# A spectral mixer and an ELU MLP on one core: unread matmuls in two start-up waits, batch 0 spread over more engines and queues, Bs reads put later in the order

## The chip, the core and the metric

The kernel runs on one core of a Trainium2 chip. The metric is the device time of one execution in microseconds, the median of several. A core has five engines with a queue each: TensorE (PE in the profile; PEld is its weight load), VectorE (DVE), ScalarE (ACT), GpSimd (POOL) and SyncE (SP). SP computes nothing here; it starts transfers. Each engine works through its instructions in the order in which the program gives them, and a wait at the head of a queue holds everything behind it. Transfers started by any engine are carried by the core's 16 DMA engines.

## The reference

```python
X = np.fft.rfft(x, axis=1)                  # x: 8 x 3008 x 256
Yr = Xr @ w_r - Xi @ w_i + b_r
Yi = Xr @ w_i + Xi @ w_r + b_i
Yr = np.sign(Yr) * np.maximum(np.abs(Yr) - 0.01, 0.0)     # softshrink, Yi alike
y = np.fft.irfft(Yr + 1j * Yi, n=3008, axis=1)
h = y.reshape(24064, 256) @ w_in            # w_in: 256 x 2048
g = np.where(h > 0.0, h, np.exp(np.minimum(h, 0.0)) - 1.0)
out = g @ w_out                             # w_out: 2048 x 256
```

## The kernel before

Two parts share the core. The first, the mixer, takes each of the 8 batches through a Fourier transform written as matmuls. Its pieces are called units. For one batch there are 8 A units (first transform stage, from a tile `xt` of the input into a bf16 tile `A`, two units to a tile), 6 X units (second stage, from `Z` to `XT`), 12 M units (the complex channel matmul, bias and softshrink, from `XT` to `Y`), 6 B units (`Y` to `Bz`) and 8 Y units (`Bs` to `yT`). A unit is a few matmuls into one PSUM tile and one evacuation of it; M has more behind it (`yb` on DVE, then `clip` and `Y`, on POOL or on ACT and DVE).

Between stages the data is transposed through DRAM: the tiles A are written to `DA` (four writes, one for every two A units) and read back as Z (12 reads), and the tiles Bz are written to `DB` (three writes) and read back as Bs (8 reads). Before the change all of these transfers are started by SP. Reads wait until the writes have landed. There are two buffers for A and two for Bz, three for Z, four for Bs, four for xt. So the evacuation of A unit 4 must wait until the write of A units 0 and 1 has landed, and that of A unit 6 for the write of units 2 and 3.

The second part is the MLP. It takes `yT` of a batch in 6 blocks of 512 columns (the last has 448), each in 8 steps, so a batch has 48 iterations (`PER`). Iteration i has `front(i)` (4 matmuls into `hps`, then an Exp on ACT), then whatever units the plan puts there, then `elu(i)` (two DVE instructions, to `gT`), then `back(i - 2)` (8 matmuls into `ps_o`; after a block's last step ACT copies the result and SP writes it out). All 8 Y units of a batch must be evacuated before the first iteration of that batch, since every Bs tile holds a part of every block.

The order is written out by hand. `plan(b)` fills the 48 iterations of batch b with X, M, B and Y units of batch b + 1 and A units of batch b + 2. Units in the loop share one PSUM tile (tag `fps`, one buffer), so a unit's matmuls wait until the unit before it has been evacuated. Batch 0 has no batch before it: its units run alone, ahead of the loop, as does the building of the transform tables `M1` to `M4` by iotas, DVE arithmetic and Sin on ACT. `plan(0)` also has to hold the A units of batch 1 (iterations 6 to 13), so it starts X of batch 1 late, at iteration 18, packs the rest, and puts all 8 Y units into iterations 45 to 47. For batches 1 to 6 (`mixed`) X starts at iteration 2, A0 stands at 24, B4 at 25, A1 and A2 at 26 and 27, B5 and all Bs reads at 28, A3 to A7 at 29 to 33 with the Z reads, and Y0 to Y7 at 38 to 45. Batch 6 has no A units, batch 7 no units at all.

Of the kernel before, what the change touches and what calls it, by code (L numbers as in the profile page):

```python
# [20 lines left out]
K1 = 24  # L21
# [4 lines left out]
def kernel(  # L26
# [88 lines left out]
    def unit_A(b, u, alone=False, on_dve=False):  # L115
# [15 lines left out]
        )  # L131
        if uu == 1:
# [3 lines left out]
            del A_of[b, ci], x_of[b, ci]  # L136

    def load_Z(b, g):
        Z = wk3.tile([P, 8, D], BF16, name="Z", tag="Z")
        for c in range(2):  # L140
            for h in range(2):
                r = h * 2 * K1 + c * K1 + 8 * g
                q = c * N2 + h * NH
                nc.sync.dma_start(Z[q : q + NH], DA_of[b][:, r : r + 8, :])
        Z_of[b, g] = Z
# [44 lines left out]
    def unit_B(b, v, alone=False, on_dve=False):  # L190
# [19 lines left out]
        )  # L210
        if v % 2:
            k0 = 8 * (v // 2)
            nc.sync.dma_start(DB_of[b][k0 : k0 + 8].rearrange("k p d -> p k d"), Bz[:])

    def load_Bs(b, w):
        Bs = wk4.tile([4 * K1, 8, D], BF16, name="Bs", tag="Bs")
        dv = DB_of[b].rearrange("k (c m) d -> (k c) m d", c=2)
        for h in range(2):
            n0 = h * NH + 8 * w
            nc.sync.dma_start(Bs[h * 2 * K1 : h * 2 * K1 + 2 * K1], dv[:, n0 : n0 + 8, :])  # L220
        Bs_of[b, w] = Bs

    def unit_Y(b, u, alone=False, on_dve=False):
# [6 lines left out]
        for j in range(8):  # L230
# [6 lines left out]
            psv[:, :, 0 : 2 * N1].rearrange("p n r -> p r n"), on_dve,  # L237
        )

    with tc.tile_pool(name="stagep", bufs=1) as stagep:  # L240
# [78 lines left out]
        r2 = stagep.tile([P, 2, 8, N2], F32, name="r2")  # L319
        for g in range(3):  # L320
            gs = slice(8 * g, 8 * g + 8)
# [9 lines left out]
            )  # L331
            for c in range(2):
                wrap(flat(v2[:, c, gs, :]), flat(r2[:, c]))
            for u in range(2 * g, 2 * g + 2):
                unit_A(0, u, alone=True)
            for c in range(2):
                nc.scalar.activation(
                    flat(M2[:, c, gs, :]), flat(v2[:, c, gs, :]), AF.Sin,
                    bias=0.0, scale=SIN_SCALE,
                )  # L340
        dume = stagep.tile([P, 1], F32, name="dume")
        nc.scalar.activation(dume[:], pcol[:], AF.Exp, scale=0.0)
        for u in range(6, 8):
            unit_A(0, u, alone=True, on_dve=(u == 7))
        for g in range(3):
            load_Z(0, g)

# [34 lines left out]
        nc.tensor.matmul(bb[:], lhsT=ones[:], rhs=brow[:], start=True, stop=True)  # L382
        nc.scalar.copy(bias_bc[:], bb[:])
        nc.gpsimd.tensor_copy(wcat_r[:, :, 0:D], w_r_f[:])
        nc.gpsimd.tensor_copy(wcat_r[:, :, D : 2 * D], w_i_f[:])
# [9 lines left out]
    def load_w(fp):  # L395
        f0 = fp * 2 * P
        wf = wk4.tile([P, 2, 2 * P], F32, name="w_in_f", tag="w_in_f")
        nc.sync.dma_start(wf[:], w_in_v[:, :, f0 : f0 + 2 * P])
        nc.gpsimd.tensor_scalar(
            w_in_s[:, :, f0 : f0 + 2 * P], wf[:], 2.0 / S, None, ALU.mult  # L400
        )
        nc.gpsimd.dma_start(w_out_r[:, 2 * fp : 2 * fp + 2, :], w_out_v[:, 2 * fp : 2 * fp + 2, :])


    unit_X(0, 0, alone=True)
    unit_X(0, 1, alone=True, on_dve=True)
    for i in range(2):
        unit_M(0, 0, i, alone=True)
    for i in range(2):
        unit_M(0, 1, i, alone=True, path="dve")  # L410
    unit_X(0, 2, alone=True)
    unit_X(0, 3, alone=True)
    for fp in range(4):
        load_w(fp)
    for i in range(2):
        unit_M(0, 2, i, alone=True, path="dve")
    unit_B(0, 0, alone=True)
    for i in range(2):
        unit_M(0, 3, i, alone=True)
    unit_B(0, 1, alone=True)  # L420
    unit_X(0, 4, alone=True)
    unit_X(0, 5, alone=True)
    for i in range(2):
        unit_M(0, 4, i, alone=True, path="dve")
    unit_B(0, 2, alone=True)
    for i in range(2):
        unit_M(0, 5, i, alone=True, path="dve")
    unit_B(0, 3, alone=True)
    unit_B(0, 4, alone=True)
    unit_B(0, 5, alone=True)  # L430
    for w in range(4):
        load_Bs(0, w)
    for fp in range(4, NPAIR):
        load_w(fp)
    for ci in range(4):
        load_x(1, ci)
    for u in range(8):
# [75 lines left out]

    def mixed(b, lead):

        r = [[] for _ in range(PER)]
        nxt = b + 1 < B
        seq = [
# [5 lines left out]
        ]  # L524
        t = lead
        for u in seq:
            if u[0] == "A":
                if not nxt:
                    t += 1
                    continue  # L530
                r[t].append(put("A", b + 1, *u[1:]))
            else:
                r[t].append(put(u[0], b, *u[1:]))
            if u == ("B", 5):
                for w in range(4):
                    r[t].append((load_Bs, (b, w)))
            if u == ("A", 7) and nxt:
                for g in range(3):
                    r[t].append((load_Z, (b + 1, g)))
            t += 1  # L540
        return r, t

    def plan(b):

        if b + 1 >= B:
            return [[] for _ in range(PER)]
        if b == 0:
            r = [[] for _ in range(PER)]
            for u in range(8):
                r[6 + u].append(put("A", 1, u))  # L550
            for g in range(3):
                r[13].append((load_Z, (1, g)))
            X = [put("X", 1, u) for u in range(6)]
            M = [[put("M", 1, q, i) for i in range(2)] for q in range(6)]
            Bu = [put("B", 1, v) for v in range(6)]
            seq = [
                [X[0]], [X[1]], [M[0][0]], [M[0][1]], [X[2]], [M[1][0]], [M[1][1]], [X[3]],
                [Bu[0]], [M[2][0]], [M[2][1], Bu[1]], [X[4]], [M[3][0]], [M[3][1], Bu[2]], [X[5]],
                [M[4][0]], [M[4][1], Bu[3]], [M[5][0]], [M[5][1], Bu[4]], [], [Bu[5]],
            ]  # L560
            t = 18
            for us in seq:
                r[t] += us
                t += 1
            for w in range(4):
                r[t - 1].append((load_Bs, (1, w)))
            for ci in range(4):
                r[15 + 4 * ci].append((load_x, (2, ci)))
            for u in range(8):
                r[t + u * 6 // 8].append(put("A", 2, u))  # L570
            for g in range(3):
                r[t + 5].append((load_Z, (2, g)))
            for u in range(8):
                r[PER - 3 + u * 3 // 8].append(put("Y", 1, u))
            return r
        r, t = mixed(b + 1, 2)
        for u in range(8):
            r[t + 4 + u].append(put("Y", b + 1, u))
        if b + 2 < B:
            for ci in range(4):  # L580
                r[3 + 4 * ci].append((load_x, (b + 2, ci)))
        return r

    n = B * PER
    todo = None
    for i in range(n + LAG):
        if i < n:
            if i % PER == 0:
                todo = plan(i // PER)
            h = front(i)  # L590
            for f, a in todo[i % PER]:
                f(*a)
            elu(i, *h)
        if i >= LAG:
            back(i - LAG)


# [28 lines left out]
```

## Time and profile before

| | us |
|---|---|
| median of 3 runs | 1074.23 (1072.34 to 1076.02) |
| the profiled execution, its own time | 1076.73 |
| span of its instructions | 1074.8 |
| PE busy | 956.4 (89%) |
| DVE busy | 829.5 (77%) |
| ACT busy | 630.7 (59%) |
| POOL busy | 259.4 (24%) |
| mean granted TensorE clock, share of 2.4 GHz | 0.95 |

The shares are means over the start-up, seven batches with units and one without, which have different limits. All rows are from that profiled execution; its times are counted from the span's start.

### The profile page before, as it was taken

The numbers are of one execution on the slowest core, as the hardware profiler recorded it, in microseconds if no ns is written. First come the engines' busy times: TensorE is split into PE (matmuls) and PEld (weight loads), VectorE is DVE, ScalarE is ACT, GpSimd is POOL, SyncE is SP. The second block draws the span as 40 slices with busy tenths as digits, with TensorE's granted clock in tenths as the row PEclk, the third lists the DMA queues.
The fourth block names the chain that finished last, engine by engine and source line by source line (L and its number), as shares of the span: only waits on it lengthen the run. The fifth ranks groups of instructions, "written<-read, shape, count | busy, mean of one in ns | idle before, by whom it ended". The sixth has DMA issues, their size and how long they took to land.

```text
span 1074.8 us, 16330 instructions
## 1 busy us (share of the span) xinstructions
PE 956.4 (89%) x6427; PEld 675.5 (63%) x6427; DVE 829.5 (77%) x932; ACT 630.7 (59%) x725; POOL 259.4 (24%) x270
## 2 busy tenths in 40 slices
PE   4648798679997999899997999899997999999997
PEld 2225575457665766577665766677665766676765
DVE  8326587528985899678985899768986888888887
ACT  4244565556675755666665756666565766565554
POOL 4415035203430055002530055101530034100000
PEclk9577899979998999999998999989999999999999
DMA  8538643641447133640536124640435211411011
GB/s 181 143 96 199 159 118 84 138 121 42 121 111 174 38 78 88 171 113 19 138 95 177 55 53 117 154 128 20 103 95 155 69 38 53 107 40 38 20 40 38
DMA packets 92784, 105.39 MB, mean 98 GB/s; under 512 B 5730, under 2 KB 83556, under 8 KB 89700
## 3 DMA queue, kind: packets, MB, share of 16 engines
q1 hardware_dynamic: 86436, 77.61, 26.4%
q0 software_dynamic: 6272, 26.74, 11.3%
q8 instruction: 50, 0.82, 0.3%
q14 instruction: 26, 0.21, 0.1%
HBM read 54.53 MB, written 49.81 MB: 97 GB/s over the span
## 4 chain that ended last, share of the span: by engine, by line
PE 69%; DVE 12%; ACT 8%; DMA 8%; issue 2%; SPq 1%; DVEq 0%; POOL 0%; ACTq 0%; POOLq 0%
PE hps L454 28%; PE ps_o L487 25%; PE mps L176 8%; DVE gT L465 8%; DMA DA<-A 6%; ACT Et L459 5%; DVE Et L463 3%; PE aps L124 3%; PE bps L200 2%; PE yps L231 2%; PE xps L155 2%; ACT A L113 1%; SPq L220 1%; DVE yb L181 1%; DMA xt<-in_x_dram 1%
## 5 line engine op out<-in xcount | busy, mean ns | idle before, releaser
L459 ACT ACTIVATE Et<-hps 128x1024 f32<-128x1024 f32 (+1 forms) x384 | 388.6, 1012 | 328.2 <-PE hps L454 325.6
L465 DVE SCALAR_TENSOR_TENSOR gT<-hps,Et 128x1024 fp32r<-128x1024 f32 (+1 forms) x384 | 461.8, 1203 | 34.9 <-DVE Et L463 0.5
L487 PE MATMUL ps_o<-w_out_r,gT 128*128 128x256 f32 (+1 forms) x3072 | 485.2, 301 | 0.7 <-DVE gT L465 0.7
L487 PEld LDWEIGHTS ps_o<-w_out_r,gT 128*128 128x128 f32 (+1 forms) x3072 | 416.2, 192 | 45.5 <-issue 10.2
L454 PE MATMUL hps<-yT,w_in_s 128*128 128x512 bf16 (+1 forms) x1536 | 399.4, 383 | 19.6 <-DVE gT L465 18.9
L463 DVE TENSOR_SCALAR Et<-Et 128x1024 f32<-128x1024 f32 (+1 forms) x384 | 280.7, 731 | 145.8 <-ACT Et L459 144.8
L184 POOL TENSOR_SCALAR clip<-yb 128x512 f32<-128x512 f32 x88 | 78.7, 894 | 590.9 <-DVE yb L181 590.5
L454 PEld LDWEIGHTS <-w_in_s 128*128 128x128 bf16 x1536 | 128.9, 99 | 138.5 <-issue 32.0
L185 POOL TENSOR_TENSOR Y<-yb,clip 128x512 bf16<-128x512 f32 x88 | 112.8, 1282 | 7.5
L124 PE MATMUL aps<-xt,M 94*96 94x512 f32 x128 | 55.0, 521 | 57.6 <-ACT A L113 44.1
L113 ACT CAST A<-aps 96x1024 bf16<-96x1024 f32 x63 | 62.9, 1003 | 55.1 <-DMA DA<-A 43.4
L181 DVE TENSOR_TENSOR yb<-mps,bias_bc 128x512 f32<-128x512 f32 x96 | 66.4, 691 | 26.6 <-PE mps L176 19.6
L176 PEld LDWEIGHTS <-XT 128*128 128x128 bf16 x384 | 38.3, 101 | 60.3 <-issue 14.6
L124 PEld LDWEIGHTS aps<-xt,M 94*96 94x96 f32 x128 | 21.4, 190 | 76.2 <-ACT A L113 57.9
L176 PE MATMUL mps<-wcat_r,XT 128*128 128x512 bf16 x192 | 61.2, 399 | 8.4 <-DVE yb L181 5.0
L176 PE MATMUL mps<-wcat_s,XT 128*128 128x512 bf16 x192 | 60.7, 399 | 0.0
L113 ACT CAST yT<-yps 128x752 bf16<-128x752 f32 x60 | 47.0, 784 | 14.5 <-PE yps L231 14.5
L113 ACT CAST Bz<-bps 128x1024 bf16<-128x1024 f32 x48 | 48.7, 1018 | 8.2 <-PE bps L200 8.2
L499 ACT COPY osb<-ps_o 128x512 f32<-128x512 f32 x96 | 50.8, 583 | 4.1 <-PE ps_o L487 4.1
L99 POOL DMA_DIRECT2D xt<-in_x_dram x64 | 44.0, 690 | 34.2 <-PE aps L124 34.0
L113 ACT CAST XT<-xps 128x1024 bf16<-128x1024 f32 x47 | 47.0, 1005 | 5.2 <-PE xps L155 5.2
L231 PE MATMUL yps<-M,Bs 96*128 96x94 bf16 x512 | 34.1, 217 | 15.7 <-DMA Bs<-DB 10.0
(69 smaller groups left out, 220.8 us busy)
## 6 DMA issues: line engine op xcount, KB each, us to landing
xt<-in_x_dram POOLq DMA_DIRECT2D x32, 640.0 KB, 6.1
out_dram<-osb SPq DMA_DIRECT2D x40, 512.0 KB, 3.1
DA<-A SPq DMA_DIRECT2D x32, 384.0 KB, 5.9
Z<-DA SPq DMA_DIRECT2D x96, 128.0 KB, 3.2
DB<-Bz SPq DMA_DIRECT2D x24, 512.0 KB, 3.2
Bs<-DB SPq DMA_DIRECT2D x64, 192.0 KB, 4.7
xt<-in_x_dram POOLq DMA_DIRECT2D x32, 112.0 KB, 5.7
out_dram<-osb SPq DMA_DIRECT2D x8, 384.0 KB, 2.6
```

What stands on the lines that cost most here:

```text
L113: nc.scalar.copy(dst, src)
L124: nc.tensor.matmul(ps[0 : 4 * K1, j, :], lhsT=M1[:], rhs=xt[:, 4 * uu + 2 * j : 4 * uu + 2 * j + 2, :], start=True, stop=True,)
L176: nc.tensor.matmul(ps[:, i, :], lhsT=XT[:, dt, c, o : o + P], rhs=wm[:, dt, :], start=(m == 0 and dt == 0), stop=(m == 1 and dt == 1),)
L181: nc.vector.tensor_tensor(yb[:], ps[:, i, :], bias_bc[:], ALU.add)
L184: nc.gpsimd.tensor_scalar(clip[:], yb[:], LAM, -LAM, ALU.min, ALU.max)
L185: nc.gpsimd.tensor_tensor(Y[:, i, :], yb[:], clip[:], ALU.subtract)
L231: nc.tensor.matmul(psv[:, j, 0 : 2 * N1], lhsT=Bs[:, j, dt * P : dt * P + P], rhs=M4[:], start=True, stop=True,)
L454: nc.tensor.matmul(hps[:, s, 0:nb], lhsT=w_in_s[:, dt, ft * P : ft * P + P], rhs=yT[:, dt, bs : bs + nb], start=(dt == 0), stop=(dt == 1),)
L459: nc.scalar.activation(Et[:, :, 0:nb], hps[:, :, 0:nb], AF.Exp)
L463: nc.vector.tensor_scalar(Et[:, :, 0:nb], Et[:, :, 0:nb], 1.0, -1.0, ALU.min, ALU.add)
L465: nc.vector.scalar_tensor_tensor(gT[:, :, 0:nb], hps[:, :, 0:nb], 0.0, Et[:, :, 0:nb], ALU.max, ALU.add)
L487: nc.tensor.matmul(po[q][0 : t1 - t0, i_ % 2, :], lhsT=gT[:, s, t0:t1], rhs=w_out_r[:, ft, :], start=(ft == 0 and i_ % 2 == 0), stop=(ft = ...
```

## The change

1. Start-up. In the table loop the A units of batch 0 alternate between ACT and DVE for their evacuation; units 6 and 7 are put ahead of the last Sins, and every unit writes its own half of the tile to DA. X units alternate likewise. The Z and Bs reads of batch 0 are started half by SP and half by ACT.
2. The M units of batch 0 alternate between the two softshrink paths. The MLP weights come in 4 large loads of `w_in`, into buffers of the loop's tiles, early, with the scaling done by DVE after unit B5, and 2 loads of `w_out`, started by POOL; `load_x` of batch 1 moves ahead of B3.
3. `idle_pe(n)` issues n matmuls whose result nobody reads: 20 ahead of X0, 22 ahead of Y0 of batch 0.
4. `plan` returns two lists. Units of `f1` stand where units stood; those of `f2` behind `back`. Bs reads stand in `f2` of the iteration of A4, Z reads in `f2` of the last A unit, and Y0 to Y7 at iterations 40 to 47 for all batches.
5. `plan(0)` gets a list of its own: X of batch 1 from iteration 17, some iterations with two units, A units of batch 2 spread over iterations 32 to 39.

```diff
+def load_Bs(b, w, engs=None):           # load_Z alike
+    engs = engs or (nc.sync, nc.sync)
...
+            engs[h].dma_start(Bs[h * 2 * K1 : h * 2 * K1 + 2 * K1], dv[:, n0 : n0 + 8, :])
...
+    def idle_pe(n):
+        ps = psO.tile([P, 512], F32, name="idle", tag="outp")
+        for _ in range(n):
+            nc.tensor.matmul(
+                ps[:], lhsT=M2[:, 0, 0:2, :].rearrange("p a b -> p (a b)"),
+                rhs=M2[:, 0, 0:8, :].rearrange("p a b -> p (a b)"), start=True, stop=True,
+            )
...
+            wrap(flat(v2[:, 0, gs, :]), flat(r2[:, 0]))
+            unit_A(0, 2 * g, alone=True)
+            unit_A(0, 2 * g + 1, alone=True, on_dve=True)
+            if g == 2:
+                unit_A(0, 6, alone=True)
+                unit_A(0, 7, alone=True, on_dve=True)
+            wrap(flat(v2[:, 1, gs, :]), flat(r2[:, 1]))
+            sines(g)
...
+    def both_M(q):
+        unit_M(0, q, 0, alone=True, path="pool")
+        unit_M(0, q, 1, alone=True, path="dve")
...
+    both_M(5)
+    load_w_out(1)
+    for ci in range(4):
+        load_x(1, ci)
     unit_B(0, 3, alone=True)
     unit_B(0, 4, alone=True)
-    unit_B(0, 5, alone=True)
+    unit_B(0, 5, alone=True, on_dve=True)
     for w in range(4):
-        load_Bs(0, w)
-    for fp in range(4, NPAIR):
-        load_w(fp)
-    for ci in range(4):
-        load_x(1, ci)
+        load_Bs(0, w, (nc.sync, nc.scalar))
+    for q in range(4):
+        nc.vector.tensor_scalar_mul(
+            w_in_s[:, :, q * FQ : q * FQ + FQ], w_in_f[q][:], 2.0 / S
+        )
+    idle_pe(22)
...
+            lead, pairs = 17, [
+                [("X", 0), ("X", 1)], [("M", 0, 0)], [("M", 0, 1)], [("X", 2), ("X", 3)],
+                [("M", 1, 0)], [("M", 1, 1)], [("M", 2, 0)], [("M", 2, 1), ("B", 0)],
+                [("X", 4), ("X", 5)], [("M", 3, 0)], [("M", 3, 1), ("B", 1)],
+                [("M", 4, 0)], [("M", 4, 1), ("B", 2)], [("M", 5, 0)], [("M", 5, 1), ("B", 3)],
+                [("A", 0)], [("A", 1), ("B", 4)], [("A", 2)], [("B", 5), ("A", 3)], [("A", 4)],
+                [("A", 5)], [("A", 6)], [("A", 7)],
+            ]
...
+        for t, us in enumerate(pairs, lead):
+            us = [u for u in us if n2 < B or u[0] != "A"]
+            at(t, *us[:1])
+            at(t, *us[1:], r=f2)
+            if ("A", 4) in pairs[t - lead]:
+                f2[t] += [(load_Bs, (n1, w)) for w in range(4)]
...
         for u in range(8):
-            r[t + 4 + u].append(put("Y", b + 1, u))
+            at(40 + u, ("Y", u))
```

In the order of SP's transfers, this is what stood around the Bs reads in the iterations of batch 1 before:

```order
L133 DMA DA<-A 96x8x256
L213 DMA DB<-Bz 128x8x256
L220 DMA Bs<-DB 48x2048 x8
L133 DMA DA<-A 96x8x256 x3
L144 DMA Z<-DA 32x2048 x12
```

And this is the same place after:

```order
L138 DMA DA<-A 96x8x256
L223 DMA DB<-Bz 128x8x256
L138 DMA DA<-A 96x8x256
L231 DMA Bs<-DB 48x2048 x8
L138 DMA DA<-A 96x8x256 x2
L534 DMA out_dram<-osb 128x4x256
L149 DMA Z<-DA 32x2048 x12
```

The second write of A (units 2 and 3) moved from behind the 8 Bs reads to ahead of them; the other two stay behind. On POOL's queue, start-up ends before with these rows, from the last two M units on its path to the loads of batch 1:

```order
L184 TENSOR_SCALAR clip<-yb 128x512
L185 TENSOR_TENSOR Y<-yb,clip 128x512
L399 TENSOR_SCALAR w_in_s<-w_in_f 128x2x256
L402 DMA w_out_r<-in_moe_w_out_dram 128x2x256
L399 TENSOR_SCALAR w_in_s<-w_in_f 128x2x256
L402 DMA w_out_r<-in_moe_w_out_dram 128x2x256
L399 TENSOR_SCALAR w_in_s<-w_in_f 128x2x256
L402 DMA w_out_r<-in_moe_w_out_dram 128x2x256
L399 TENSOR_SCALAR w_in_s<-w_in_f 128x2x256
L402 DMA w_out_r<-in_moe_w_out_dram 128x2x256
L99 DMA xt<-in_x_dram 80x2048
L99 DMA xt<-in_x_dram 14x2048
```

and after with these:

```order
L189 TENSOR_SCALAR clip<-yb 128x512
L190 TENSOR_TENSOR Y<-yb,clip 128x512
L434 DMA w_out_r<-in_moe_w_out_dram 128x8x256
L99 DMA xt<-in_x_dram 80x2048
L99 DMA xt<-in_x_dram 14x2048
```

The scalings of w_in, which waited for loads that SP starts behind the Bs reads, are gone from POOL, so nothing on its queue holds the loads of batch 1 back once the last clip is done.

## Rows read from the trace of the kernel before

**Rows 1.** Windows, one per batch, between first Exps; ACT instructions of L459 alone.
```profile
core 0: us, ACT busy (x), PEclk, DMA share, GB/s
89.33:243.91 154.58, 48.49 (x48) 0.90 0.53 130
243.91:367.06 123.15, 48.60 (x48) 0.97 0.40 102
...
735.23:856.76 121.53, 48.62 (x48) 0.99 0.37 97
856.76:968.88 112.12, 48.63 (x49) 1.00 0.20 57
968.88:1074.82 105.94, 48.48 (x48) 0.99 0.10 34
```

**Rows 2.** Windows of a few iterations each, cut at Exp starts; same columns.
```profile
89.33:103.20 13.87, 6.16 (x6) 0.76 0.77 177
968.88:981.46 12.58, 6.16 (x7) 1.00 0.12 38
973.07:1052.69 79.62, 39.05 (x38) 1.00 0.10 33
...
375.91:381.28 5.37, 2.06 (x3) 1.00 0.00 0
440.79:447.64 6.85, 3.08 (x4) 1.00 0.74 205
447.64:459.55 11.91, 2.05 (x3) 0.79 0.70 177
164.24:168.59 4.35, 1.02 (x1) 1.00 0.30 66
226.02:243.91 17.89, 2.75 (x3) 0.81 0.44 111
```

**Rows 3.** Waits: engine and line, what it waited for; us, times, longest.
```profile
ACT A L113 <- DMA DA<-A: 43.4, 8, 6.4
```

**Rows 4.** Timeline around one long wait, batch 2: start, us, instruction, idle before.
```profile
440.18 0.37 SPq L213 DMA_DIRECT2D DB<-Bz  x1
...
441.71 1.00 ACT L113 CAST A<-aps 96x1024 bf16<-96x1024 f32 x1
...
444.22 3.77 SPq L220 DMA_DIRECT2D Bs<-DB  x8
...
446.28 1.00 ACT L113 CAST A<-aps 96x1024 bf16<-96x1024 f32 x1
...
448.08 9.37 SPq L133 DMA_DIRECT2D DA<-A  x3
...
453.85 1.01 ACT L113 CAST A<-aps 96x1024 bf16<-96x1024 f32 x1 [5.18 <-DMA DA<-A]
```

**Rows 5.** DMA issues from 440 to 460 us: KB each, median us to landing.
```profile
Bs<-DB SPq DMA_DIRECT2D x8, 192.0 KB, 4.1
```

**Rows 6.** Windows of start-up, X0 to the last evacuation of B5, and its two parts.
```profile
core 0: us, PE busy (x) PEld busy (x) DVE busy (x) ACT busy (x) POOL busy (x), PEclk, DMA share, GB/s
33.32:72.78 39.46, 28.17 (x144) 12.00 (x144) 15.34 (x21) 15.97 (x19) 16.37 (x16) 0.67 0.35 93
33.32:55.08 21.76, 17.39 (x68) 7.45 (x69) 8.61 (x11) 6.55 (x8) 12.66 (x12) 0.50 0.51 132
55.08:72.78 17.70, 10.78 (x77) 4.55 (x75) 6.74 (x10) 9.42 (x12) 3.71 (x4) 0.89 0.16 44
```

**Rows 7.** Timeline of start-up: TensorE's last work ahead of X0, and X0 and X1.
```profile
27.16 1.41 PE L382 MATMUL bb<-brow,ones 1*128 1x512 f32 x2
...
33.32 1.87 PE L155 MATMUL xps<-M,Z 128*128 128x128 bf16 x16 [4.75 <-DMA Z<-DA]
```

**Rows 8.** The chain that ended last, 60 to 95 us: start, us, what.
```profile
62.24 1.88 PE mps L176 x4
...
72.78 3.22 DMA DB<-Bz
...
79.29 5.99 DMA Bs<-DB
```

**Rows 9.** The chain that ended last, 100 to 125 us.
```profile
107.43 11.81 DMA DA<-A
```

More of the change, by code (lines that the diff above doesn't have):

```diff
@@ L131, in unit_A @@
         )
-        if uu == 1:
+        if alone:
+            n0 = 4 * u
+            nc.sync.dma_start(
+                DA_of[b][n0 : n0 + 4].rearrange("n r d -> r n d"), A[:, 4 * uu : 4 * uu + 4, :]
+            )
+        elif uu == 1:
             nc.sync.dma_start(
@@ L319, with sines @@
         r2 = stagep.tile([P, 2, 8, N2], F32, name="r2")
+        def sines(g):
+            gs = slice(8 * g, 8 * g + 8)
+            for c in range(2):
+                nc.scalar.activation(
+                    flat(M2[:, c, gs, :]), flat(v2[:, c, gs, :]), AF.Sin,
+                    bias=0.0, scale=SIN_SCALE,
+                )
         for g in range(3):
@@ L331 @@
             )
[L332 to L340, printed above, removed]
+            wrap(flat(v2[:, 0, gs, :]), flat(r2[:, 0]))
[6 more added lines that the diff above has]
+            sines(g)
         dume = stagep.tile([P, 1], F32, name="dume")
         nc.scalar.activation(dume[:], pcol[:], AF.Exp, scale=0.0)
-        for u in range(6, 8):
-            unit_A(0, u, alone=True, on_dve=(u == 7))
         for g in range(3):
-            load_Z(0, g)
+            load_Z(0, g, (nc.sync, nc.scalar))
         ident_b = stagep.tile([P, P], BF16, name="ident_b")
@@ L393 @@
     w_out_v = moe_w_out.rearrange("(t p) e -> p t e", p=P).bitcast(F32R)
[L395 to L402, printed above, removed]
+    FQ = DFF // 4
+    w_in_f = []
@@ new lines, in load_w_in, with load_w_out @@
+    def load_w_in():
+        for q in range(4):
+            if q < 3:
+                wf = late3.tile([P, 2, FQ], F32, name="w_in_f", tag="Et")
+            else:
+                wf = late2.tile([P, 2, FQ], F32, name="w_in_f", tag="osb")
+            nc.sync.dma_start(wf[:], w_in_v[:, :, q * FQ : q * FQ + FQ])
+            w_in_f.append(wf)
+    def load_w_out(hh):
+        hf = slice(hh * NFT // 2, (hh + 1) * NFT // 2)
+        nc.gpsimd.dma_start(w_out_r[:, hf, :], w_out_v[:, hf, :])
+    def both_M(q):
+        unit_M(0, q, 0, alone=True, path="pool")
+        unit_M(0, q, 1, alone=True, path="dve")
@@ L405 @@
     unit_X(0, 0, alone=True)
     unit_X(0, 1, alone=True, on_dve=True)
[L407 to L410, printed above, removed]
+    load_w_in()
+    both_M(0)
+    load_w_out(0)
+    both_M(1)
     unit_X(0, 2, alone=True)
-    unit_X(0, 3, alone=True)
-    for fp in range(4):
-        load_w(fp)
-    for i in range(2):
-        unit_M(0, 2, i, alone=True, path="dve")
+    unit_X(0, 3, alone=True, on_dve=True)
+    both_M(2)
@@ L417 @@
     unit_B(0, 0, alone=True)
-    for i in range(2):
-        unit_M(0, 3, i, alone=True)
+    both_M(3)
     unit_B(0, 1, alone=True)
     unit_X(0, 4, alone=True)
-    unit_X(0, 5, alone=True)
-    for i in range(2):
-        unit_M(0, 4, i, alone=True, path="dve")
+    unit_X(0, 5, alone=True, on_dve=True)
+    both_M(4)
     unit_B(0, 2, alone=True)
-    for i in range(2):
-        unit_M(0, 5, i, alone=True, path="dve")
+    both_M(5)
+    load_w_out(1)
+    for ci in range(4):
+        load_x(1, ci)
@@ L428 @@
     unit_B(0, 3, alone=True)
     unit_B(0, 4, alone=True)
-    unit_B(0, 5, alone=True)
+    unit_B(0, 5, alone=True, on_dve=True)
     for w in range(4):
-        load_Bs(0, w)
-    for fp in range(4, NPAIR):
-        load_w(fp)
-    for ci in range(4):
-        load_x(1, ci)
+        load_Bs(0, w, (nc.sync, nc.scalar))
+    for q in range(4):
+        nc.vector.tensor_scalar_mul(
+            w_in_s[:, :, q * FQ : q * FQ + FQ], w_in_f[q][:], 2.0 / S
+        )
+    idle_pe(22)
     for u in range(8):
@@ L512, in put @@
         return ({"A": unit_A, "X": unit_X, "M": unit_M, "B": unit_B, "Y": unit_Y}[kind], (b, *a))
[L514 to L518, printed above, removed]
[5 rows of a table removed]
[L524 to L541, printed above, removed]
@@ L543, in plan, with at @@
     def plan(b):
+        f1 = [[] for _ in range(PER)]
+        f2 = [[] for _ in range(PER)]
         if b + 1 >= B:
-            return [[] for _ in range(PER)]
+            return f1, f2
+        n1, n2 = b + 1, b + 2
+        def at(t, *us, r=f1):
+            for u in us:
+                r[t].append(put(u[0], n2 if u[0] == "A" else n1, *u[1:]))
         if b == 0:
-            r = [[] for _ in range(PER)]
             for u in range(8):
-                r[6 + u].append(put("A", 1, u))
-            for g in range(3):
-                r[13].append((load_Z, (1, g)))
@@ L553, in plan @@
[L553 to L559, printed above, removed]
-            ]
-            t = 18
@@ L575, in plan @@
-            return r
-        r, t = mixed(b + 1, 2)
-        for u in range(8):
-            r[t + 4 + u].append(put("Y", b + 1, u))
[L579 to L582, printed above, removed]
+                f1[6 + u].append(put("A", 1, u))
+            f1[13] += [(load_Z, (1, g)) for g in range(3)]
+            lead, pairs = 17, [
[6 rows of a table added]
+            ]
+            xs = (15, 18, 21, 24)
+        else:
+            lead, pairs = 2, [[u] for u in (
[5 rows of a table added]
+            )]
+            xs = (3, 7, 11, 15)
@@ new lines, in plan @@
+        for t, us in enumerate(pairs, lead):
[4 more added lines that the diff above has]
+                f2[t] += [(load_Bs, (n1, w)) for w in range(4)]
+        if n2 < B:
+            f2[t] += [(load_Z, (n2, g)) for g in range(3)]
+            for ci in range(4):
+                f1[xs[ci]].append((load_x, (n2, ci)))
+        for u in range(8):
+            at(40 + u, ("Y", u))
@@ L588 @@
             if i % PER == 0:
-                todo = plan(i // PER)
+                f1, f2 = plan(i // PER)
             h = front(i)
-            for f, a in todo[i % PER]:
+            for f, a in f1[i % PER]:
                 f(*a)
@@ L595 @@
             back(i - LAG)
+        if i < n:
+            for f, a in f2[i % PER]:
+                f(*a)
 _INS = ['x', 'w_r', 'w_i', 'b_r', 'b_i', 'moe_w_in', 'moe_w_out']
```

31 lines of the change are left out of this document (12 added, 19 removed), and 10 rows, old and new, of tables (seq, xs).

## The prediction

> **What bounds the kernel now.** I began with the span cut into batches [rows 1]. Batch 7, which has no units, takes 105.94 us, and 38 of its iterations take 79.62 us, 2.095 each [rows 2]: that is the floor of the loop. A batch with units is not far above it where nothing goes wrong: batch 6, which lacks only the A units, takes 112.12. Batches 1 to 5 take 612.85 together (from 243.91 to 856.76, 122.57 each), batch 0 takes 154.58, and start-up 89.33. So three places hold what is left to get: start-up, batch 0, and about ten microseconds in each of five batches.
>
> The list of waits names the last: ACT, evacuating an A unit, waited 43.4 us in 8 waits for writes of A to DRAM [rows 3]. The timeline of one of them shows why [rows 4]. ACT has A unit 3 in its tile at 442.71 (start 441.71 and 1.00), and the write of that tile could start there. SP has the 8 Bs reads ahead of it, though, and these wait for the write of Bz that was started at 440.18; SP starts them from 444.22 to 447.99, and the write of A only at 448.08. It lands some 5.8 later, and unit 6, which needs that buffer, is evacuated at 453.85 after 5.18 idle. Two iterations take 11.91 in that stretch at a mean granted clock of 0.79, where undisturbed iterations with an A unit take 2.283 (6.85 for three) [rows 2]: the excess is 11.91 - 4.57 = 7.34. The clock loss of the restart is inside it.
>
> **The change, part by part.**
>
> *Batches 1 to 5.* The second write of A now stands ahead of the Bs reads, so it starts at about 442.7 on that timeline. Unit 6 can be evacuated one A iteration after unit 5, 446.28 + 2.28 = 448.56 [rows 2, 4]. That leaves 5.85 for a write that took 5.8 behind all eight reads; now it has only the tail of the Bz write ahead of it and the reads after it. I take the wait as gone. If nothing new appears, that is 5 x 7.34 = 36.7 off, 115.2 for a batch; batch 6 plus 8 A units at 2.283 - 2.095 each comes to 113.6, which agrees within 1.6. The upper bound of what is left: the write shares the engines with the Bs reads and lands with the last of them. These would start from 444.3 to 448.1 and land 4.1 later [rows 5], at 452.2; a wait of 3.6, and 3.6 x 7.34 / 5.18 = 5.1 with the clock loss, 25.5 over five. The writes of units 4 to 7 go behind the Bs reads, with nothing but the Z reads late by it, and X uses these from iteration 2 of the next batch, some 16 iterations on; the Bs reads themselves come one or two iterations later for a Y0 that moved two iterations later too.
>
> *The batch boundary.* Y7 now stands in iteration 47, and the next `front` needs its evacuation. No single Y there is shown. Nothing is the lower bound, as one unit beside `back` may be covered; the upper one is the end of batch 0, where 8 Y units in three iterations took 17.89 [rows 2], so 11.6 over 3 x 2.095, or 1.45 each. I take 0.3 at each of 6 boundaries, 1.8, near the low end because a single unit has no other unit to queue behind.
>
> *Batch 0.* With the same units and single Y units it should cost a clean batch, 115.2, with additions: the 8 A units of batch 1, 8 x 0.19 = 1.5; a start at a low clock, 13.87 for six iterations against 12.58 for the same six of batch 7 [rows 2], 1.3; and nine iterations with two units. A pair ahead of `back` (M and B) took 4.35 [rows 2]; M alone takes 2.685 (5.37 for two), and a light unit adds about 0.19, so 2.87 would be the price of no collision, and 1.48 is the excess. The second of a pair now stands behind `back`, whose matmuls cover part of the wait for the shared PSUM buffer, so I take 0.7, between the ends: 6.3. Sum: 124.3, 30.3 less than 154.58, with 118 and 131 as the ends. It assumes that the write of batch 1's first A tiles, 11.81 us at 107.43 [rows 9], gets short. It ran among the loads of x for batches 1 and 2, and the loads of batch 1 now start during start-up; with a landing of about 5.8, as above, three A iterations (6.85) cover it.
>
> *Start-up.* Three parts, the least certain ones. First, X0 begins at 33.32, behind TensorE's last matmul at 28.57 [rows 7]. Three more evacuations of about 1 us on DVE delay the last tables by about 3, to 31.6, and 20 unread matmuls come on top. A 512-column matmul took 0.47 at the half clock (1.88 for four) [rows 8], so 20 take 4.7 to 9.4, and the X units queue behind them on TensorE although Z has landed. I take 6: X0 at 37.6. The ends are 33.3 (the wait hides all) and 41.
>
> Second, from X0 to the last evacuation of B5, 39.46 [rows 6]. TensorE is busy for 17.39 at 0.50 and 10.78 at 0.89 of the clock, so 18.3 at full clock, and not busy for 11.3: M's second half waits for `yb`, the first M of a pair waits for XT. With X evacuated on two engines I take 10 of these, and a clock of 0.8, between the 0.67 of that stretch and full: 18.3 / 0.8 + 10 = 33. The ends are 28 (full) and 46 (half). So B5 is done at 70.6 instead of 72.78. Neither softshrink path nor the w_out load on POOL counts: POOL and ACT are busy for 16 of 39 us. The rule in the Trainium skill (TensorE: Matmul & The Clock Gate, Part 1) is that the throttled clock is the default and activity releases it. The half clock ahead of 55.08, with TensorE busy 17.39 of 21.76, speaks against trusting that here. By the rule the sum would be that of the third rival, and by the row the one above.
>
> Third, from B5 to the first Exp, 16.55 before (72.78 to 89.33). Half of the Bs reads move to ACT's queue, which saves half of SP's 3.77 [rows 4], 1.9. Against it, the last half of w_out and the loads of x for batch 1 are now on the DMA engines during the write of Bz, 3.22, and the Bs reads, 5.99 to land [rows 8]. The write of A that met such loads took 11.81 instead of 3 or so, so the price lies between 0 and 8.6; I take 3, about a third, since the second half of M and three B units lie between the start of these loads and the last write, and part of the loads is through by then. The scaling of w_in on DVE falls into this wait. So do the 22 unread matmuls (5.2 to 10.3). So 17.7, and the first Exp at 88.3, 1.0 earlier. The ends are 77 and 97.
>
> *Sum*, on the profiled span: 1074.8 - 36.7 + 1.8 - 30.3 - 1.0 = 1008.6. That execution's own time was 1.9 above its span, and the median of the runs is 2.5 below that execution, so 1008.
>
> **Rivals.**
>
> *The write of A still lands late.* It has a head start of only about 1.5 us over the Bs reads. With the wait of 3.6 above, 18 to 25 come back: 1026 to 1033. For it: 5.85 of room for a write that took 5.8 is thin. Against it: those 5.8 had all the reads ahead of it. The Trainium skill says the like (DMA: Bandwidth & Descriptors, Issuing engines are not separate DMA queues): transfers of any issuing engine end up on the same 16 DMA engines and interleave. That the wait doesn't shrink at all would take SP being held by something else ahead of the write: 1045.
>
> *Batch 0 keeps its waits.* Pairs at 1.48 instead of 0.7 add 7, and one wait for a write of A of the size above adds 7.3: 1022. For it: the pairs' shared PSUM buffer. Against it: no Bs read stands ahead of its early writes.
>
> *The unread matmuls hold the clock.* X0 at 36.3, 28 us to B5 and 17 to the first Exp, 81: 1001. For it: the stretch from 55.08 at 0.89. Against it: 11 us of gaps.
>
> *Y in the narrow block costs what it cost in a pile.* If each of the 56 Y units took 1.45 in the last block, ahead of the boundary, the change would add 81 and give back 68.0: 1088, slower. It decides from 1.21 us for a Y. Against it: batch 6, 112.12, has 48 x 2.095 = 100.6 of plain iterations and 12 M at 0.59, which leaves 4.5 for 20 units, 8 single Y units among them.
>
> **How the numbers follow.** Forecast 0.66, between 992 and 1021; late write 0.11; batch 0 keeping its waits 0.10; the clock held 0.06; no shrinking at all 0.03; Y in the narrow block 0.02; something that cancels all of it 0.02. The range 988 to 1032 takes in the first four but for their tails, some 12 in 100 left out. Below 0.3%, 3 us, two results of this kernel can't be told apart. Faster by more than that: 0.96; the same: 0.01; slower: 0.03.
>
> **What would show it.** Right: no ACT wait of several microseconds for DA in batches 1 to 5, each near 115.5; batch 0 near 124; first Exp near 88; X0 later than before, with unread matmuls ahead of it. Wrong: a wait for DA that is left in iteration 32; Exp gaps at the batch boundaries; paired iterations above 4; Bs reads that take ten microseconds or more to land in start-up.

## The result, and the profile after

The changed kernel takes 1031.07 us (median of 4 runs, 1027.77 to 1032.89) against 1074.98 for the kernel before in the runs beside it: a ratio of 0.9592 with a 95% interval of 0.9558 to 0.9625. Faster was forecast, and the time lies inside the stated range, but only just: it is 23 above the predicted 1008 and 1 below the upper end of 1032, and two of the four executions lie beyond that end. The profiled execution is the fastest of the four; its own time is 1027.77 and its span 1025.8, 49.0 below the span before.

The windows by batch, cut at the starts of the Exps (line 493 now) as in [rows 1], show where those 49 us came from:

```profile
core 0: us, ACT busy (x), PEclk, DMA share, GB/s
104.11:229.56 125.45, 48.65 (x48) 0.99 0.51 128
229.56:345.06 115.50, 48.63 (x48) 1.00 0.43 109
...
691.58:807.09 115.51, 48.61 (x48) 1.00 0.39 102
807.09:919.80 112.71, 48.59 (x48) 1.00 0.20 56
919.80:1025.82 106.02, 48.46 (x48) 0.99 0.10 34
```

| | before | predicted | after | difference |
|---|---|---|---|---|
| start-up (to the first Exp) | 89.33 | 88.3 | 104.11 | +14.8 |
| batch 0 | 154.58 | 124.3 | 125.45 | -29.1 |
| batches 1 to 5 | 612.85 | 577.6 | 577.53 | -35.3 |
| batch 6 | 112.12 | 112.4 | 112.71 | +0.6 |
| batch 7 | 105.94 | 105.9 | 106.02 | +0.1 |

The loop came out within 2 us of its forecast. Start-up missed by 16, towards slower.

Three stretches of batch 0 hold its gain: iterations 10 to 12, 42, and 45 to 47. These are their windows, before and then after (columns as above), and between them what ACT waited for in iteration 42 before:

```profile
112.81:128.18 15.37, 3.10 (x3) 0.78 0.63 171
208.32:220.98 12.66, 0.95 (x2) 0.65 0.85 205
226.02:243.91 17.89, 2.75 (x3) 0.81 0.44 111
...
215.49 1.01 ACT L113 CAST A<-aps 96x1024 bf16<-96x1024 f32 x1 [6.22 <-DMA DA<-A]
...
126.34:133.21 6.87, 3.13 (x4) 1.00 0.71 191
216.72:218.52 1.80, 0.96 (x1) 1.00 0.54 155
222.84:229.56 6.72, 2.76 (x3) 1.00 0.35 105
```

They are 8.5, 10.9 and 11.2 us shorter, 30.5 together; the other iterations came out 1.4 longer.

**The wait that went.** The timeline around the same place in batch 2, beside [rows 4]:

```profile
417.09 1.01 ACT L113 CAST Bz<-bps 128x1024 bf16<-128x1024 f32 x1
...
418.12 0.37 SPq L223 DMA_DIRECT2D DB<-Bz  x1
419.65 1.00 ACT L113 CAST A<-aps 96x1024 bf16<-96x1024 f32 x1
...
420.68 0.33 SPq L138 DMA_DIRECT2D DA<-A  x1
421.93 1.00 ACT L113 CAST A<-aps 96x1024 bf16<-96x1024 f32 x1
...
422.97 3.78 SPq L231 DMA_DIRECT2D Bs<-DB  x8
424.22 0.99 ACT L113 CAST A<-aps 96x1024 bf16<-96x1024 f32 x1
...
426.50 1.00 ACT L113 CAST A<-aps 96x1024 bf16<-96x1024 f32 x1
```

A unit 3 is evacuated at 419.65 and its write starts at 420.68, right behind it and 2.29 ahead of the first Bs read. Units 4, 5 and 6 follow at 421.93, 424.22 and 426.50, a steady 2.28 apart: unit 6 finds its buffer free. The write lands 3.3 us after its start, with 5.8 of room. The list of waits has no row any more of ACT waiting for DA, where [rows 3] had 43.4 us, and the granted clock of these batches is 1.00.

**The wait that came.** The chain that ended last in start-up, beside [rows 8]:

```profile
72.03 1.24 DVE Bz L111
...
73.28 17.96 DMA DB<-Bz
...
92.16 6.70 DMA Bs<-DB
...
98.90 2.71 PE yps L242 x32
```

B5 is evacuated at 73.27, near the 72.78 of before, but its write to DRAM takes 17.96 instead of 3.22. The DMA queues in ten microseconds of that wait (packets, MB, share of 16 engines):

```profile
DMA packets 738, 2.47 MB, mean 247 GB/s; under 512 B 101, under 2 KB 459, under 8 KB 459
...
q0 software_dynamic: 380, 2.29, 95.2%
q1 hardware_dynamic: 358, 0.18, 23.3%
```

q0 holds the loads of x (and up to about 77 us the end of the w_out load), q1 the last three writes of Bz, 256 KB each. They get nearly the same number of packets, 380 and 358, and thirteen times different bytes: a packet of q0 has 6 KB on average, one of Bz 0.5 KB. When q0 was all but dry, at 88 us, the other queue got through most of what was left, two thirds of its 0.79 MB, in two microseconds:

```profile
DMA packets 1046, 0.54 MB, mean 269 GB/s; under 512 B 55, under 2 KB 1042, under 8 KB 1042
...
q1 hardware_dynamic: 1026, 0.51, 93.8%
q0 software_dynamic: 20, 0.03, 6.8%
```

That is not the whole of the wait. From 73.28 to 76 the trace has 550 packets of q0 and none of q1, though writes of Bz had been started. Why the turns began only behind that, no run here shows.

**The unit phase.** The windows from X0 to the end of B5, whole and in two parts, beside [rows 6]:

```profile
core 0: us, PE busy (x) PEld busy (x) DVE busy (x) ACT busy (x) POOL busy (x), PEclk, DMA share, GB/s
35.49:73.27 37.78, 27.54 (x152) 12.05 (x151) 17.11 (x23) 11.66 (x14) 16.07 (x20) 0.73 0.43 119
35.49:54.23 18.74, 12.96 (x68) 5.88 (x67) 7.96 (x11) 4.27 (x6) 6.58 (x7) 0.73 0.60 169
54.23:73.27 19.04, 14.59 (x86) 6.17 (x85) 9.14 (x13) 7.39 (x9) 9.49 (x13) 0.73 0.27 70
```

It takes 37.78 instead of 39.46; 33 was predicted. The timeline has the unread matmuls ahead of it, and one pass of its chain:

```profile
31.16 4.49 PE L255 MATMUL idle<-M 128*128 128x512 bf16 x20
...
35.49 1.06 PE L160 MATMUL xps<-M,Z 128*128 128x128 bf16 x16
...
41.33 0.72 ACT L192 ACTIVATE clip<-yb,lam_n 128x512 f32<-128x512 f32 x1 [4.18 <-DVE yb L186]
...
42.08 0.69 DVE L193 SCALAR_TENSOR_TENSOR Y<-yb,clip 128x512 bf16<-128x512 f32 x1 [0.79 <-ACT clip L192]
...
42.69 0.68 DVE L186 TENSOR_TENSOR yb<-mps,bias_bc 128x512 f32<-128x512 f32 x1
...
43.43 0.59 PE L181 MATMUL mps<-wcat_r,XT 128*128 128x512 bf16 x2 [2.00 <-DVE yb L186]
...
44.57 1.91 PE L160 MATMUL xps<-M,Z 128*128 128x128 bf16 x16
```

The 20 unread matmuls ran at full clock (0.22 each) and X0 followed at full clock (1.06 for 16). From 43.99 the clock was granted at half (1.2 GHz), so the next 16 matmuls of an X unit took 1.91. Between lies the gap: DVE waits 0.79 for ACT's clip, then does Y, then the next yb, and TensorE stands 2.00 for that.

### The profile page after: what moved, and what is told of

Its sections match the earlier page's. It is cut to its first block, busy times and chain, and to the rows that moved or that the text cites. A ratio compares the mean times of both kernels' runs of the same rounds, so it can differ in the third digit from the quotient of the medians.

```text
span 1025.8 us, 16436 instructions
## 1 busy us (share of the span) xinstructions
PE 943.5 (92%) x6469; PEld 662.4 (65%) x6469; DVE 835.1 (81%) x940; ACT 620.9 (61%) x717; POOL 246.6 (24%) x260
## 4 chain that ended last, share of the span: by engine, by line
PE 69%; DVE 15%; ACT 10%; DMA 4%; issue 2%; DVEq 0%; ACTq 0%; POOL 0%; POOLq 0%
PE hps L488 27%; PE ps_o L521 23%; PE mps L181 9%; DVE gT L499 8%; ACT Et L493 7%; DVE Et L497 4%; PE aps L124 3%; PE bps L205 2%; PE yps L242 2%; PE xps L160 2%; DMA DB<-Bz 2%; ACT osb L533 1%; DMA DA<-A 1%; DMA xt<-in_x_dram 1%; ACT XT L113 1%
## 5 line engine op out<-in xcount | busy, mean ns | idle before, releaser
L521 PE MATMUL ps_o<-w_out_r,gT 128*128 128x256 f32 (+1 forms) x3072 | 472.4, 296 | 1.8 <-ACT osb L533 1.1
L521 PEld LDWEIGHTS ps_o<-w_out_r,gT 128*128 128x128 f32 (+1 forms) x3072 | 403.2, 186 | 46.0 <-issue 7.8
L488 PE MATMUL hps<-yT,w_in_s 128*128 128x512 bf16 (+1 forms) x1536 | 392.5, 377 | 22.4 <-DVE gT L499 20.2
L190 POOL TENSOR_TENSOR Y<-yb,clip 128x512 bf16<-128x512 f32 x90 | 115.7, 1285 | 7.5
L113 ACT CAST A<-aps 96x1024 bf16<-96x1024 f32 x60 | 60.1, 1001 | 8.4 <-PE aps L124 8.2
L124 PE MATMUL aps<-xt,M 94*96 94x512 f32 x128 | 50.5, 483 | 15.7 <-DMA xt<-in_x_dram 13.7
L242 PEld LDWEIGHTS <-Bs 96*128 96x128 bf16 x512 | 30.0, 104 | 31.0 <-DMA Bs<-DB 20.1
```

Source lines behind the costliest of these rows:

```text
L113: nc.scalar.copy(dst, src)
L124: nc.tensor.matmul(ps[0 : 4 * K1, j, :], lhsT=M1[:], rhs=xt[:, 4 * uu + 2 * j : 4 * uu + 2 * j + 2, :], start=True, stop=True,)
L190: nc.gpsimd.tensor_tensor(Y[:, i, :], yb[:], clip[:], ALU.subtract)
L242: nc.tensor.matmul(psv[:, j, 0 : 2 * N1], lhsT=Bs[:, j, dt * P : dt * P + P], rhs=M4[:], start=True, stop=True,)
L488: nc.tensor.matmul(hps[:, s, 0:nb], lhsT=w_in_s[:, dt, ft * P : ft * P + P], rhs=yT[:, dt, bs : bs + nb], start=(dt == 0), stop=(dt == 1),)
L521: nc.tensor.matmul(po[q][0 : t1 - t0, i_ % 2, :], lhsT=gT[:, s, t0:t1], rhs=w_out_r[:, ft, :], start=(ft == 0 and i_ % 2 == 0), stop=(ft = ...
```

## The experiments

**Early loads of x.** Theory: the large packets of x hold up the write of Bz. Rival: the smaller writes and the two queues do.

```diff
     load_w_out(0)
+    for ci in range(4):
+        load_x(1, ci)
     both_M(1)
...
     both_M(2)
+    load_w_out(1)
     unit_B(0, 0, alone=True)
...
-    load_w_out(1)
-    for ci in range(4):
-        load_x(1, ci)
     unit_B(0, 3, alone=True)
```

> The changed kernel, with the loads of x for batch 1 started on POOL's queue right behind the first half of w_out, and the second half of w_out behind M unit 2, so that these 4.1 MB have landed before the last writes of Bz. Theory: the write of the last Bz took 17.96 us in start-up (3.22 before the change) because its small packets took turns with the large packets of these loads. Then it lands in 3 to 4 again, the Bs reads are started near 77 instead of 91.3, the first Exp comes near 89.5 instead of 104.1, and the whole is 14 to 15 us shorter than the changed kernel, near 1016. Rival: the write is slow because the Bz writes of batch 0 were cut into halves and half of the Bs reads moved to ACT's queue. Then it stays above 10 us and the time stays within 3 of 1031.

Measured: 1015.50 us, a ratio of 0.9448 (0.9399 to 0.9498). The chain that ended last has the write short again, though it is still cut in halves and half of the reads are still started by ACT:

```profile
74.70 2.60 DMA DB<-Bz
...
78.69 7.97 DMA Bs<-DB
```

The first Exp comes at 90.65. The theory holds in size too: the first Exp is 13.5 us earlier in the profiles, and the medians are 15.6 apart.

**x late, w_out early.** How much of it is x, and is it a matter of turns or of bytes?

```diff
     both_M(2)
+    load_w_out(1)
...
-    load_w_out(1)
     for ci in range(4):
         load_x(1, ci)
```

> The changed kernel with the second half of w_out moved ahead and the loads of x for batch 1 left where the change put them. Theory (packet by packet): a small packet of Bz is served for each large packet of x, so the last write of Bz lands only about when the 3.1 MB of x are through, 11 to 14 us after its start. Rival (an equal share of bytes for both queues): 0.75 MB of Bz is through when 1.5 MB have moved, 6 to 7 us after its start.

One run: 1024.40; the first Exp at 100.71. The write took, by the chain that ended last:

```profile
73.37 14.68 DMA DB<-Bz
```

An equal share of bytes is excluded; the write took longer than even the 11 to 14 of the theory. q0 was all but empty at 85, and the write landed 3 us later, as in the changed kernel (88 and 91.24). Taking w_out away saved 3.3 us of the 18.

**No unread matmuls.** The changed kernel without `idle_pe(20)` and `idle_pe(22)`.

> The changed kernel without the 42 unread matmuls. Theory: they do not hold the clock through the unit phase, which fell to half at 43.99 with them; the 20 ahead of X0 delay it by about 2 us (35.49 to near 33.4), the 22 ahead of Y0 end at 76.84 while Y0 begins at 95.49, and so change nothing. X0 earlier by 2 and the first ten microseconds of the units at half clock, slower by 2 to 4: the time stays within 3 us of 1031. Rival (by the rule that activity holds the clock): without them the units run at half clock throughout, and the last evacuation of B5 comes 6 us later or more, near 1037.

Measured: 1027.70, 0.9563 (0.9513 to 0.9614), which overlaps with the changed kernel's interval. X0 starts at 32.73, 2.76 earlier, and B5 ends at 71.99, 1.28 earlier. The unit phase, without the 42 and then in the run of the next paragraph, whose start-up is that of the kernel before:

```profile
32.73:71.99 39.26, 26.86 (x141) 11.91 (x144) 17.01 (x23) 12.25 (x15) 15.25 (x19) 0.87 0.46 124
```

```profile
33.33:71.72 38.39, 26.15 (x141) 11.75 (x144) 15.32 (x21) 15.96 (x19) 16.37 (x16) 0.90 0.36 94
```

The rival is refuted: without unread matmuls the mean granted clock is 0.87, not half, and higher than the 0.73 with them. But one execution can't give the effect on the clock: the same start-up had 0.67 in the kernel before and 0.90 in that run, with phases of 39.46 and 38.39. What stands is that the 42 bought nothing that the time shows.

**The Bs move alone.** The kernel before, with one edit in `mixed` (`nxt` is false for the last batch, which has no A units to place):

```diff
             if u[0] == "A":
+                if nxt:
+                    r[t].append(put("A", b + 1, *u[1:]))
+                if u == ("A", 4):
+                    for w in range(4):
+                        r[t].append((load_Bs, (b, w)))
                 if not nxt:
...
-                r[t].append(put("A", b + 1, *u[1:]))
             else:
...
-            if u == ("B", 5):
-                for w in range(4):
-                    r[t].append((load_Bs, (b, w)))
```

> The kernel before, with one part of the change alone: the Bs reads of batches 2 to 7 are started in the iteration of A4 instead of that of B5. Theory: this one move takes away the wait of ACT for DA, 7.34 us in each of five batches; the kernel before gets 36 to 37 us shorter, near 1038. Rival: the two lists, Z reads behind back and Y units two iterations later are needed too; then 20 us or less come off.

Measured: 1036.86, 0.9657 (0.9586 to 0.9727), so 38 to 39 off. Batches 1 and 5, by windows between Exps:

```profile
242.99:358.09 115.10, 48.63 (x49) 1.00 0.43 109
703.49:818.59 115.10, 48.63 (x49) 1.00 0.40 103
```

All of the gain of batches 1 to 5 is this one place in SP's order. They are even 0.4 shorter than in the changed kernel. Batch 0, which the edit leaves alone, still takes 155.16.

**The Bs reads put back.** The changed kernel with the reads of batches 2 to 7 in the iteration of B5.

```diff
-            if ("A", 4) in pairs[t - lead]:
+            if ("A" if b == 0 else "B", 4 if b == 0 else 5) in pairs[t - lead]:
                 f2[t] += [(load_Bs, (n1, w)) for w in range(4)]
```

> The changed kernel with the Bs reads of batches 2 to 7 put back into the iteration of B5, all else as changed. Theory: the wait of ACT for the second write of A comes back in batches 1 to 5, 5 to 7.4 us each, 1031 becomes 1056 to 1068. Rival: the wait went for another reason (f2, Y or Z reads later); then the time stays within 5 of 1031.

Measured: 1066.69, 0.9924 (0.9898 to 0.9950). Batches 1 to 5 take 122.3 to 123.6 again, and the list of waits has the row back:

```profile
ACT A L113 <- DMA DA<-A: 28.6, 5, 6.5
```

**Early loads, no unread matmuls.** Both edits together.

> The kernel of the run with the early loads of x, without the 42 unread matmuls. Theory: the 20 cost 2 to 4 us at X0; the 22 now end 3.4 us before the first Bs lands and hold the clock for two of the four Y pairs, worth about 1.5 us. Together 1012 to 1015 against 1015.5. Rival (activity ahead of work pays): 1018 or more.

Measured: 1012.35, 0.9408 (0.9386 to 0.9431), which overlaps with 0.9448; the first Exp at 89.69 instead of 90.65. Again nothing for the 42: in both pairs the median is lower without them, by 3.4 and 3.2 us, so if anything they cost time.

**Reads by SP alone.** With the early loads of x, Z and Bs of batch 0 are started by SP again.

> The kernel of the run with the early loads of x, with the Z and Bs reads of batch 0 all started by SP again. Theory: ACT's half of the issues saves about 1.8 us ahead of the last Bs, so the first Exp comes 1.5 to 2 us later (near 92.5), and Z is hidden by the unread matmuls: 1017. Rival (the same 16 DMA engines carry them, so the issue time is hidden behind the transfers): the first Exp stays within 0.7 of 90.65.

Measured: 1017.22, 0.9447 (0.9423 to 0.9470): the totals can't be told apart. In the profiles the start of the last write of Bz and the first Exp are 17.45 us apart (74.38 to 91.83) against 15.95 (74.70 to 90.65), and 16.17 in the run with Y one iteration earlier, which has the partner's start-up. So the second queue saves 1.3 to 1.5, where 1.9 was put in the sum. The first Exp by itself doesn't decide it: it came at 91.83 here and at 91.82 in that other run.

**Softshrink held.** Early loads, no unread matmuls, and the Y instruction of the ACT path is issued on DVE behind the next unit's yb: `shrink` issues it, and `let_go` calls what is held.

```diff
-            nc.vector.scalar_tensor_tensor(Y[:, i, :], yb[:], LAM, clip[:], ALU.add, ALU.min)
...
+            held.append(shrink)
+            if not hold:
+                let_go()
...
     def both_M(q):
         unit_M(0, q, 0, alone=True, path="pool")
-        unit_M(0, q, 1, alone=True, path="dve")
+        let_go()
+        unit_M(0, q, 1, alone=True, path="dve", hold=True)
```

> The kernel of the run with early loads and no unread matmuls, and on DVE the last softshrink instruction of each M unit of batch 0 that takes the ACT path stands behind the next M unit's yb instead of ahead of it. Theory: in the unit phase (37.8 us instead of the 33 predicted) DVE stands six times for 0.85 us waiting for ACT's clip and then works 0.7 on Y, while TensorE waits for the next yb behind it; taking the clip, its wait and Y out of that chain shortens each of six M pairs by 1.2 to 1.6, 7 to 9 us in all, near 1006. Rival: the phase is set by TensorE at half clock, and the chain only fills time in which it would be busy or waiting anyway; then 2 us or less.

Measured: 1011.16, 0.9391 (0.9361 to 0.9421), not to be told from 1012.35. The phase shrank from 40.1 (X0 at 33.33, last write of Bz at 73.43) to 37.5 (33.18 to 70.70). That is 2.6 of the 7 to 9 expected, and not even these are shown to be the chain's: the granted clock of the phase was 0.62 in the partner's profile and 0.82 in this one. At 0.73 the changed kernel, with the chain, took 37.78, and the unfilled kernel below, without it, 37.55. So the theory was wrong. What set the pace instead is not shown by this run.

**Filled gaps.** The held softshrink, with unread matmuls put where TensorE waits.

```diff
     def both_M(q):
+        if q % 2 == 0:
+            idle_pe(7)
         unit_M(0, q, 0, alone=True, path="pool")
         let_go()
+        idle_pe(3)
         unit_M(0, q, 1, alone=True, path="dve", hold=True)
```

Beside these there are 8 ahead of X0 and 22 ahead of Y0.

> The kernel of the run with the held softshrink, with unread matmuls put into the gaps themselves: 8 ahead of X0, 7 ahead of M units 0, 2 and 4 (where TensorE waits for XT), 3 between the two halves of each M (where it waits for yb), 22 ahead of Y0. Theory: the unit phase is set by TensorE at half clock, which falls because of the gaps; with the gaps filled the granted clock stays at full from X0 to B5 and the phase takes 29 to 31 us instead of 37.5, the first Exp comes 6 to 8 us earlier, total 1003 to 1005. Rival: waiting for DVE and ACT sets the phase whatever the clock, and unread matmuls stand in the way of read ones; then the time is 1010 or more.

Measured: 1010.40, 0.9397 (0.9353 to 0.9441), not to be told from 1011.16: no gain in time. The clock did stay at full (2.4 GHz) up to 55.69, but something else stood in the way. The timeline of POOL, and of DVE in the same place:

```profile
50.74 0.51 POOL L99 DMA_DIRECT2D xt<-in_x_dram  x1 [4.69 <-DMA w_out_r<-in_moe_w_out_dram]
51.28 0.62 POOL L195 TENSOR_SCALAR clip<-yb 128x512 f32<-128x512 f32 x1
```

```profile
53.28 1.29 DVE L192 TENSOR_TENSOR yb<-mps,bias_bc 128x512 f32<-128x512 f32 x2 [5.86 <-POOL Y L196]
```

POOL waited 4.69 at its eighth load of x until w_out had landed. The clip of M's softshrink stood behind that, the three buffers of yb ran out, and DVE waited 5.86; TensorE, waiting for yb in turn, stood 3.96 and started again at 54.63, and the clock fell behind that. The same stop of POOL was 2.17 in the run with the held softshrink. The time is that of the rival, but its cause is not the one that the rival names.

**Y one iteration earlier.** With the early loads of x, Y at 39 to 46.

> The kernel of the run with the early loads of x, with the Y units at iterations 39 to 46 instead of 40 to 47. Theory: Y7's evacuation stands between the last iteration of a batch and the first of the next and costs 0.3 us; batches 1 to 5 come to 115.2 instead of 115.53, 2 us in all over 7 boundaries. Rival: the third of a microsecond only moves, since a unit costs that anywhere; then the batches stay within 0.1 of 115.53.

One run: 1013.28. Batches 1 and 5 by windows:

```profile
218.81:333.70 114.89, 48.63 (x49) 1.00 0.43 109
678.40:793.30 114.90, 48.62 (x49) 1.00 0.39 103
```

So 0.64 less than the 115.53 of its partner: the boundary costs twice what I took. Batch 0 gained nothing by it, 127.0 as in its partner: its last iteration is shorter, but iteration 39, where Y0 now meets the last A unit, took 4.28 instead of 2.19.

**x held back, gaps filled; and the same unfilled.** The second half of w_out and the loads of x wait on POOL for the last Bs tile, Y at 39.

```diff
+    gate = constp.tile([1, D], F32, name="gate")
+    nc.gpsimd.tensor_copy(gate[:], Bs_of[0, 3][0:1, 0, :])
+    load_w_out(1)
+    for ci in range(4):
+        load_x(1, ci)
```

> The kernel of the run with filled gaps, with the second half of w_out and the loads of x for batch 1 held on POOL until the last Bs tile of batch 0 has landed (a copy of one of its rows on POOL stands ahead of them), and Y at iterations 39 to 46. Theory: in the run with filled gaps POOL stood 4.69 us at its eighth load of x, M's next softshrink behind it, and TensorE lost 4 us at 50 to 54; without that the unit phase takes 30 to 31 us, the first Exp comes at 81 to 82, each of batches 1 to 6 is 0.6 shorter, and the whole comes to 1000 to 1003. Rival: the loads of x now collide with the first A units of batch 1 and a wait of several us appears in iterations 6 to 13; then 1006 or more.

> The same kernel without any unread matmul. Theory: the granted clock falls in the gaps of the unit phase as in the run with the held softshrink, the phase takes 36 to 37 us, and the whole comes 5 to 7 us above its partner with the gaps filled. Rival: unread matmuls are worth nothing here either way; then the two stay within 2 us of each other.

Measured: filled 1003.57, 0.9337 (0.9315 to 0.9359); unfilled 1006.94, 0.9364 (0.9342 to 0.9386). The windows from X0 to the end of B5, filled and then unfilled:

```profile
35.06:66.02 30.96, 28.48 (x192) 13.47 (x191) 16.91 (x23) 11.66 (x14) 12.95 (x13) 1.00 0.49 140
```

```profile
33.00:70.55 37.55, 26.42 (x144) 11.66 (x144) 16.88 (x23) 12.24 (x15) 13.10 (x13) 0.73 0.46 127
```

The granted clock is 1.00 against 0.73 and the phase 6.6 shorter; the first Exp comes at 81.31 against 85.78, 4.5 earlier and not 6.6, since X0 waits for the unread matmuls ahead of it. In the medians the two are 3.4 apart, less than the 5 to 7 of the theory and more than the 2 of the rival, and their intervals against the kernel before overlap. The clock is no accident of the profiled executions: over the whole kernel it is 0.992 to 0.994 in the four filled ones and 0.978 to 0.990 in the five unfilled ones. The other rival, a wait in iterations 6 to 13, didn't come: iterations 10 to 12 took 6.9 us as in the changed kernel. The filled one is the fastest kernel of this study, 71 us below the kernel before, and 0.6 above the 1000 to 1003 expected.

## Why the prediction was right, and where it failed

*Batches 1 to 5:* right in mechanism and size. The wait of 7.34 each was read from one place in SP's order. The move alone took it off, putting it back brought it back. The rival of the late write didn't happen: unit 6 came 2.28 after unit 5, and the write landed in 3.3 us, where the room was 5.85.

*Batch 0:* 125.45 against 124.3, right as a sum. Two of the three stretches that hold the gain were named, the late first write of A and the pile of Y units. The third, 10.9 us in iteration 42, was another wait for a write of A; the prediction names no wait there, and the sum has this gain only because it starts from a batch without waits. Of the prices, four iterations with an M and a B took 3.32 each, where 3.57 was put; the one with X0 and X1 took 4.67, above the 4 named as a sign of wrong; and the slow start of 1.3 didn't come (12.59 for the first six iterations). That they cancel is luck in part.

*The boundary:* right in kind, and 0.3 was too little. Batch 6 is 0.6 longer, and Y one iteration earlier takes 0.64 off a batch.

*Start-up* is the step that failed, in its third part: 17.7 predicted from B5 to the first Exp, 30.84 measured (73.27 to 104.11). I gave the collision of the write of Bz with the loads of x a price of 3 and an upper bound of 8.6, from a write of A that met other such loads, 11.81 us [rows 9]; measured, it is 14.7, the 17.96 less the 3.22 of before. I had argued that part of the loads would be through by the time of the last write. They were started from 69.34, 3.9 us ahead of it, but only 0.55 of their 4.13 MB had moved by then. The other 3.58 moved while the write waited; while the write of A in [rows 9] waited, 2.15 MB of such loads did. Both waited the loads out, so the bound was the time of the loads and not the longest wait seen before: an estimate from their 4.13 MB and the 247 GB/s above is 16.7 us. The Trainium skill has the rule (DMA: Bandwidth & Descriptors, Queues, rings and completion order): each DMA engine goes round its queues a packet at a time. The trace agrees from 76 to 86 us, with 380 packets against 358, as the profile counts them, for 2.29 MB against 0.18. It doesn't explain the 3 us ahead of that without a packet of q1.

*The second part* was mis-sized: 33 predicted, 37.78 measured. At the clock of 0.73 instead of the 0.8 that I took, the 18.3 at full clock become 25.1, 2.2 more. Most of the rest is in the gaps: they come to 10.2, but the busy time counts 1.35 us at the end (from 71.92) in which only unread matmuls ran, so without these they are 11.6, near the 11.3 of before, where I took 10. *The first part* was 2 too long (X0 at 35.49, not 37.6), as the 20 matmuls ran at full clock in that execution, 4.49 for all. In three later runs with the same 20 they took 6 to 7, and X0 came at 37.86 to 38.81.

*The rival of the held clock* was wrong for this change. Unread matmuls ahead of the phase didn't hold the clock through it: it fell at 43.99, behind a gap of 2.00. Put into the gaps they held it at 1.00. The Trainium skill (TensorE: Matmul & The Clock Gate, Part 1) says that activity releases the throttle. The filled and the unfilled kernel agree with that, 1.00 against 0.73; what these runs add is that the matmuls had to stand where the gaps are.

What stays open: why one execution takes 1027.77 and another 1032.89 us. Part of it may be the granted clock of the unit phase and of the matmuls ahead of X0, which differed between profiles of one and the same start-up.

## What to carry to other kernels

Read a queue's order as closely as an engine's: one move of eight reads behind one write was worth 36 us here, because a read that waits at the head of a queue holds back a write that was ready. When a bulk load is moved ahead to be out of the way, see which short transfer on the critical path now runs beside it, and how many bytes of that load are still to come: here the short one, of small packets, waited until the whole load was through, in 14.68 and 17.96 us. Unread matmuls kept TensorE's clock here only where its gaps were, and elsewhere delayed what stood behind them. And a difference in clock between two profiles is no effect of an edit until it is seen against profiles of the same code: 0.67 and 0.90 here.

## What I had not expected of the hardware

The last of three 256 KB writes took 17.96 us beside large loads and 2.6 without them; its queue got 7% of the bytes that moved between 76 and 86 us, with nearly half of the packets.

POOL, starting transfers one after another, stopped for 4.69 us at the eighth load of x behind one of w_out, until that w_out load had landed, and the arithmetic behind it on that engine stopped with it. In the run with x late and w_out early, where that load had landed long before, eight loads of x in a row went out without a stop. Whether the chip or the program's own semaphores make the ninth transfer wait for the first, no run here shows.
